# One more quarter of the first matrix by seven products, and two sums begun by a copy from bank to bank

## The chip, the cores and the metric

The kernel runs on one core of a Trainium2 chip. The metric is the device time of one execution in microseconds (us). The core's engines work side by side, each through a list of its own, and wait for one another by semaphores: TensorE (PE in the profile; its weight loads are PEld), VectorE (DVE), ScalarE (ACT), GpSimd (POOL) and SyncE (SP). The last two only start transfers here, apart from one table that POOL makes at the beginning.

## The reference

Attention with a window feeds a two-matrix layer whose activation is `h - tanh(h)`:

```python
# attention: 4 x 8 heads, 768 positions, 64 wide
scores = q @ k.T / 8 - slope[head] * dist          # kept: the 96 last positions and the 8 first ones
x = softmax(scores) @ v                            # 3072 tokens x 512
# layer
h = x @ w_in                                       # 512 -> 2048
g = h - np.tanh(h)
out = g @ w_out                                    # 2048 -> 512
```

Inputs and output are float32; the kernel multiplies in bf16 and adds up in float32.

## The kernel before

The 3072 tokens are cut into 24 tiles of 128, numbered 0 to 23 in the kernel's own order. Each goes through attention (S: scores, E: exp on ScalarE, M: mask by VectorE, AV: product with the values, R and N: division by the row sum, Xe: transposed into `xT`), then through the first matrix, `h - tanh(h)` into `gall` (th on ScalarE, g on VectorE), and the second matrix, and is stored (st).

**First matrix.** Tiles are taken in groups: 0 and 1 alone, then five pairs (groups 2 to 6), then three groups of four tiles (7: tiles 12 to 15, 8: 16 to 19, 9: 20 to 23). The 2048 columns are 16 blocks of 128. For a group of four tiles `m1.g.f` makes one block: four matmuls of 512 columns at line 477, added up in one bank. Groups 8 and 9 make blocks 4 to 15 in another way: a *unit* (g, j) is a quarter of the matrix, blocks 4j to 4j+3, and is worked out by the seven products of Strassen and Winograd (`d1` to `d7`, line 536, four matmuls of 256 columns each) on 2 x 2 blocks. They need sums of weights (`v1` to `v4` for each j, line 509) and of inputs (`y1` to `y4` for each g, line 514). A unit has three banks, r, q and z. Bank r takes M1, then M6, M5 and M3 on top, and ScalarE copies its state after M1, M6 and M5 (`e0`, `e1`, `e2`); q takes M2; z takes M7 and M4. VectorE makes the results from banks and copies: `q11` (M2 plus the copy of M1, in bank q), `q22` and `q21` (z plus a copy). Tanh and g then take two blocks at a time from two banks or from memory, 1024 elements wide (lines 562 and 568), against 512 for an m1 (lines 576 and 590).

**Second matrix.** For each pair of tiles a, a+1 the same scheme (`p1` to `p7`, line 645, eight matmuls of 256 columns each), with sums of activations made by VectorE (`n1` to `n4`, line 630) and of weights (`w1` to `w4`). Copies of bank r are `a0`, `a1`, `a2`; results are `c11` (q plus the copy of M1), `c12` (a copy of r), `c21` and `c22` (z plus a copy), each 128x256 (line 659, copies at 274 and 276).

**What sets the order.** ORDER is a list of some 980 words, written out in the file; the kernel takes them one by one and gives each to its engine (`/a` ScalarE, `/d` VectorE, `/p` POOL, `/s` SP where the operation has a choice). Nothing is moved afterwards, so an engine's list is the words of that engine in this order, and an instruction that waits holds up all behind it on its engine. HOMES gives each value its bank, its piece of the common memory `mem` or its buffer. The time of a wait thus follows from both lists. Loads of q, k and v (lq, lk, lv) are started by POOL, transposing transfers (T, Xe) by SP, stores by either.

Of the kernel before, what the change touches and what calls it, by code (L numbers as in the profile page):

```python
# [29 lines left out]
lv.6 a1.0/a c11.0 th.3.0 w3.0 p5.0 g.3.10 p7.0 a2.0/a n1.2/d th.3.4 g.3.0 p1.2 th.3.6 n2.2/d p2.2 a0.2/a w4.1 th.3.8  # L30
c22.0 p6.2 V.5/a n4.2/d T.8 p4.0 n3.2/d a1.2/a g.3.8 T.9 p5.2 g.3.6 p7.2 c21.0 a2.2/a T.10 g.3.4 st.1.0/p p3.2 M.6.1
lk.11 c11.2 S.7 c12.2/a c22.2 lv.11 n4.0/d AV.6 E.7.1 p4.2 lk.12 R.6 N.6/d E.7.0 m1.3.14 lv.9 K.7/d V.6/d M.7.1 X.6
lk.16 th.3.14 p3.0 M.7.0 Xe.6/a c21.2 lq.11 AV.7 g.3.14 c12.0/a lk.13 R.7 S.8 N.7/d lq.12 n1.4/d X.7 E.8.1 p1.4 Xe.7/d
lv.10 n2.4/d m1.4.8 K.9/a E.8.0 v1.1 st.2.0/p n3.4/d m1.4.10 th.4.8 a0.4/d lv.8 g.4.8 p6.4 th.4.10 v2.1 E.9.0 lq.13
m1.4.14 g.4.10 M.8 a1.4/a S.9 th.4.14 T.11 p5.4 g.4.14 E.9.1 V.7/d p2.4 a2.4/d E.10.0 M.9 T.12 m1.4.2 E.10.1 n4.4/d
m1.4.6 K.10/a st.0.0/s M.10 AV.9 th.4.6 m1.4.0 th.4.2 g.4.6 m1.4.4 R.9 T.13 N.9/d p7.4 g.4.2 th.4.4 Xe.9 th.4.0 g.4.4
AV.8 V.9/a p3.4 c11.4 c22.4 R.8 m1.4.12 N.8/d c12.4/a st.4.0/p g.4.0 p4.4 Xe.8 th.4.12 lq.15 v3.1 S.10 c21.4 lk.15
g.4.12 p1.6 E.12.0 lv.13 n1.6/d p2.6 n2.6/d a0.6/a lq.14 E.11.1 K.12/d AV.10 lk.14 p6.6 E.11.0 R.10 c11.6 V.10/d lq.16
m1.5.10 N.10/d a1.6/a K.11/a n4.6/d lv.12 S.11 th.5.10 n3.6/d T.15 p5.6 g.5.10 E.12.1 v1.3 m1.5.8 E.13.1 M.12 m1.5.14
a2.6/a th.5.8 T.14 M.11 m1.5.12 E.13.0 m1.5.6 v3.3 th.5.12 Xe.10 v4.1 th.5.14 g.5.12 p3.6 th.5.6 g.5.8 T.16 AV.11 g.5.14  # L40
m1.5.2 g.5.6 m1.5.0 V.11/d th.5.2 R.11 N.11/d c12.6/a p7.6 th.5.0 st.6.0/p g.5.2 Xe.11 lk.17 AV.12 g.5.0 m1.5.4 c22.6
# [11 lines left out]
lv.21 g.7.14 m1.7.13 th.7.0 T.23 g.7.11 p4.10 g.7.0 th.7.13 Xe.19 g.7.13 S.16 v4.2 p1.12 c21.10 E.20.0 K.21/d n1.12/d
p2.12 K.20/d a0.12/d E.21.0 n2.12/d AV.18 E.20.1 c11.12 p6.12 R.18 N.18/d a1.12/a n1.14/d S.17 Xe.18 n3.12/d p5.12 M.20
E.21.1 Xe.16 p7.12 a2.12/a n4.12/d E.22.0 AV.20 c22.12 p3.12 M.21 E.22.1 p4.12 K.22/a c12.12/a R.20 n2.14/d V.20/a
st.12.0/p S.18 n3.14/d lv.23 p1.14 N.20/d E.23.1 M.22 AV.21 E.23.0 d1.8.1 d2.8.1 y1.8 e0.8.1/a R.21 p2.14 y2.8 a0.14/a
N.21/d V.21/a d6.8.1 y3.8 Xe.21 AV.22 q11.8.1 e1.8.1/a m1.8.0 R.22 c21.12 N.22/d Xe.20 d5.8.1 th.8.0 d7.8.1 c11.14
e2.8.1/a y4.8 d1.8.3 g.8.0 Xe.22 d2.8.3 e0.8.3/a q22.8.1 d3.8.1 d6.8.3 M.23 th.8.4 st.11.0/s d1.8.2 p6.14 e0.8.2/a
n4.14/d V.22/a d6.8.2 g.8.4 e1.8.3/a d2.8.2 e1.8.2/a d4.8.1 q11.8.3 d5.8.3 AV.23 q21.8.1 e2.8.3/a d5.8.2 a1.14/a R.23
q11.8.2 d3.8.3 e2.8.2/a d7.8.3 N.23/d th.8.12 d3.8.2 q22.8.3 Xe.23 p5.14 th.8.6 g.8.12 d7.8.2 a2.14/a st.13.0/s m1.8.2  # L60
q22.8.2 st.8.0/s th.8.8 p3.14 g.8.6 d4.8.3 g.8.8 th.8.2 d4.8.2 c12.14/a m1.9.0 st.14.0/p y1.9 q21.8.3 m1.8.1 g.8.2
th.8.14 d1.9.1 q21.8.2 m1.8.3 e0.9.1/a y2.9 th.8.10 g.8.14 p7.14 d1.9.2 c22.14 th.8.1 d6.9.1 y3.9 d2.9.2 g.8.10 e1.9.1/a
d2.9.1 th.8.3 p4.14 g.8.1 e0.9.2/a g.8.3 d5.9.1 d6.9.2 q11.9.1 p1.16 e1.9.2/a n1.16/d e2.9.1/a d5.9.2 c21.14 a0.16/a
# [58 lines left out]
def kernel(  # L122
# [11 lines left out]
    nc = tc.nc  # L134
# [249 lines left out]
    def mask_of(u, o):  # L384
        return 2 if o else min(nth[u], 1)
# [457 lines left out]
```

## Time and profile before

| what | before |
|---|---|
| median of three runs | 201.43 us (201.39 to 201.97) |
| span of the profiled execution, first to last instruction | 199.8 us |
| PE busy | 193.1 us (97%), 2219 matmuls |
| VectorE busy | 178.6 us (89%), 348 instructions |
| ScalarE busy | 135.1 us (68%), 234 instructions |
| granted TensorE clock | 1.000 throughout |
| chain that ended last, PE's share | 85% |

The profile gives the span of its execution; the three times are of runs of the whole program and lie 1.6 us above it in the median (201.43 - 199.8). A time predicted from rows of the trace is worked out against the span, and the 1.6 us are added. Rows of groups name line, engine, operation, target and source, shapes and count, then the busy time and the mean duration of one in ns, and then the idle time of the engine ahead of them with what ended it. Rows of the chain and of the timeline give start and length in us. Rows by stretch give the length, then PE, PEld, DVE, ACT and POOL busy with instruction counts, the granted clock, the transfer engines' busy share and GB/s.

### The profile page before, as it was taken

Reading aid. Unit: us, or ns where it says so; the run is one execution under the profiler, and the core shown is the slowest. Engines: PE = TensorE matmul, PEld = TensorE weight load, DVE = VectorE, ACT = ScalarE, POOL = GpSimd, SP = SyncE. Lnnn points to the kernel's source line nnn. Section 1 sums busy time; section 2 is a strip of 40 time slices with the busy share of each in tenths; the row PEclk is TensorE's granted clock in tenths of the full one; section 3 lists DMA queues with packets and bytes.
Section 4 is the critical chain, followed back from the end, with each engine's and each line's share of the span. In section 5 each row is a group of like instructions: output and inputs, shape, how many; then the busy total and the mean of one; then the engine's idle time right before and its main releaser. Section 6 shows DMA issues by size and latency. Waiting matters only on the chain.

```text
span 199.8 us, 5524 instructions
## 1 busy us (share of the span) xinstructions
PE 193.1 (97%) x2219; PEld 157.8 (79%) x2219; DVE 178.6 (89%) x348; ACT 135.1 (68%) x234; POOL 75.3 (38%) x97
## 2 busy tenths in 40 slices
PE   8799999999999999999999999999999999999992
PEld 2469998888888988988898655688898687888892
DVE  6487599999999999999999898999999999999942
ACT  3698898726569559758947789578778777464220
POOL 8987576350694057069207904702000100001110
PEclk9999999999999999999999999999999999999999
DMA  5999999999999999989996998994733101001233
GB/s 148 211 180 185 198 163 207 201 156 141 193 167 196 178 153 135 133 188 171 137 158 146 140 173 192 154 155 85 55 108 121 66 0 54 3 0 52 107 132 131
DMA packets 103545, 27.36 MB, mean 137 GB/s; under 512 B 93920, under 2 KB 101472, under 8 KB 103520
## 3 DMA queue, kind: packets, MB, share of 16 engines
q0 software_dynamic: 74048, 16.78, 89.5%
q1 hardware_dynamic: 28928, 9.70, 27.6%
q10 hardware_dynamic: 544, 0.52, 1.0%
q8 instruction: 17, 0.28, 0.5%
q14 instruction: 8, 0.07, 0.1%
HBM read 27.26 MB, written 6.29 MB: 168 GB/s over the span
## 4 chain that ended last, share of the span: by engine, by line
PE 85%; DVE 7%; DMA 3%; ACT 2%; issue 1%; ACTq 0%; DVEq 0%
PE ps L645 36%; PE ps L477 27%; PE ps L536 9%; PE ps L396 5%; PE ps L427 5%; DMA f<-in_q_dram 3%; DVE gall L590 2%; DVE x L444 2%; DVE mem L407 1%; PE ps L455 1%; ACT mem L403 1%; PE ps L320 1%; ACT mem L274 1%; PE ps L365 1%; ACT th L576 1%
## 5 line engine op out<-in xcount | busy, mean ns | idle before, releaser
L477 PE MATMUL ps<-xT,w_in_bf 128*128 128x256 bf16 (+2 forms) x544 | 69.0, 279 | 0.0
L477 PEld LDWEIGHTS <-w_in_bf 128*128 128x128 bf16 x544 | 47.2, 98 | 12.4
L576 ACT ACTIVATE th<-ps 128x512 f32<-128x512 f32 (+1 forms) x74 | 41.8, 591 | 18.7 <-PE ps L477 13.6
L590 DVE TENSOR_TENSOR gall<-ps,th 128x512 bf16<-128x512 f32 (+1 forms) x74 | 47.4, 668 | 6.0 <-ACT th L576 5.6
L645 PEld LDWEIGHTS <-gall 128*128 128x128 bf16 x488 | 46.4, 98 | 7.0
L662 POOL DMA_DIRECT2D out_dram<-ot x14 | 8.1, 580 | 102.5 <-ACT ot L274 52.4
L403 ACT ACTIVATE mem<-ps 128x1024 bf16<-128x1024 f32 x44 | 43.3, 1024 | 4.3 <-PE ps L396 4.2
L645 PE MATMUL ps<-w_out_bf,gall 128*128 128x256 bf16 (+1 forms) x296 | 36.3, 270 | 0.0
L274 ACT COPY sn<-ps 128x256 f32<-128x256 f32 x32 | 12.0, 375 | 20.3 <-PE ps L645 16.3
L645 PE MATMUL ps<-f,ss 128*128 128x256 bf16 x192 | 24.9, 273 | 0.0
L645 PE MATMUL ps<-wc,gall 128*128 128x256 bf16 x192 | 24.9, 273 | 0.0
L342 POOL DMA_DIRECT2D vb<-in_v_dram x24 | 21.5, 900 | 2.2 <-issue 1.0
L645 PEld LDWEIGHTS <-ss 128*128 128x128 bf16 x192 | 18.3, 98 | 2.8
L342 POOL DMA_DIRECT2D mem<-in_k_dram x20 | 17.9, 899 | 4.8 <-DMA w_out_bf<-in_moe_w_out_dram 3.1
L342 POOL DMA_DIRECT2D mem<-in_q_dram x20 | 18.1, 904 | 3.8 <-DMA w_out_bf<-in_moe_w_out_dram 3.0
L412 DVE TENSOR_TENSOR mem<-mem,mk 128x2048 bf16<-128x2048 bf16 x16 | 19.2, 1215 | 0.0
L659 DVE TENSOR_TENSOR ot<-ps,sn 128x256 f32<-128x256 f32 x36 | 14.7, 415 | 3.6 <-ACT sn L274 2.5
L444 DVE TENSOR_TENSOR x<-ps,rden 128x512 bf16<-128x512 f32 x23 | 15.8, 687 | 0.5
L274 ACT COPY mem<-ps 128x512 f32<-128x512 f32 (+1 forms) x22 | 12.7, 585 | 5.1 <-PE ps L536 3.9
L427 PEld LDWEIGHTS <-mem 128*128 128x128 bf16 x352 | 13.4, 97 | 2.1 <-ACT mem L403 0.5
L427 PE MATMUL ps<-vb,mem 128*128 128x65 bf16 x352 | 14.7, 193 | 0.0
L396 PE MATMUL ps<-mem 64*128 64x128 bf16 x352 | 13.1, 217 | 0.0
(78 smaller groups left out, 220.7 us busy)
## 6 DMA issues: line engine op xcount, KB each, us to landing
out_dram<-ot POOLq DMA_DIRECT2D x14, 256.0 KB, 2.8
vb<-in_v_dram POOLq DMA_DIRECT2D x24, 128.0 KB, 6.2
mem<-in_q_dram POOLq DMA_DIRECT2D x22, 128.0 KB, 6.3
mem<-in_k_dram POOLq DMA_DIRECT2D x22, 128.0 KB, 6.1
out_dram<-ot SPq DMA_DIRECT2D x9, 256.0 KB, 2.0
w_out_bf<-in_moe_w_out_dram POOLq DMA_DIRECT2D x4, 512.0 KB, 10.7
w_in_bf<-in_moe_w_in_dram POOLq DMA_DIRECT2D x4, 256.0 KB, 7.6
w_in_bf<-in_moe_w_in_dram POOLq DMA_DIRECT2D x2, 512.0 KB, 11.0
```

The lines of the kernel that those rows point to most:

```text
L274: nc.scalar.copy(out=out, in_=in_)
L342: eng(e).dma_start(out=dst, in_=rows_of(src, u).rearrange("h p d -> p h d"))
L396: nc.tensor.matmul(bank(("s", u, o), hh)[:, p * P : (p + 1) * P], buf(("qk", back[u] if o else u))[r, 1, p, :], buf(("qk", u))[r, 0, p, :] ...
L403: nc.scalar.activation(d, banks(("s", u, o), 0, 1), AF.Exp, bias=0.0, scale=scale)
L412: nc.vector.tensor_tensor(out=t, in0=t, in1=mk[:, 1:3], op=ALU.mult)
L427: nc.tensor.matmul(t[:, h // (H // 2), h % (H // 2), :], buf(("p", u, o))[:, slot(h), :], buf(("v", back[u] if o else u))[:, h, 0 : Dh + 1 ...
L444: nc.vector.tensor_tensor(out=buf(("x", u)).rearrange("q (a h) d -> q a h d", a=2), in0=t[:, :, :, 0:Dh], in1=rden.to_broadcast([P, 2, H / ...
L477: nc.tensor.matmul(t[:, (f - f0) * n : (f - f0 + 1) * n], w_in_bf[j][:, c, fo : fo + P], x[:, c, 0:n], start=(c == 0), stop=(c == CD - 1),)
L536: nc.tensor.matmul(t[:, r * 2 * P : (r + 1) * 2 * P], w(r)[:, c], x[:, c], start=first and r + c == 0, stop=c == 1, skip_group_check=not f ...
L576: nc.scalar.activation(h_view(buf(("th", g, f0)), g, m), h_view(bank(("h", g, f0)), g, m), AF.Tanh, bias=0.0, scale=1.0)
L590: nc.vector.tensor_tensor(out=o, in0=v(h), in1=v(th), op=ALU.subtract)
L645: nc.tensor.matmul(bank((holder, a))[:, c0:c1], s(f), t(f)[:, c0:c1], start=first and f == 0, stop=f == HF - 1, skip_group_check=not first,)
```

## The change

Four things are changed, and a fifth follows from them.

- Groups 8 and 9 make blocks 0 to 3 by seven products too: two more units, (8, 0) and (9, 0), in place of `m1.8.0` to `m1.8.3` and `m1.9.0` to `m1.9.3`.
- In all eight units `e0` copies M1 from bank r to bank q, on ScalarE, and `d2` adds M2 onto it with `start` off. The sum `q11` is gone, and so are the buffers `k0`.
- In the second matrix the same is done for the pairs from tile 14 on (FORKED): `a0` copies from bank r to bank q on ScalarE, `p2` adds onto it, and `c11` becomes a copy out of bank q, by ScalarE (pairs 16, 18, 20) or VectorE (14, 22).
- The scores set `start` only on the first of the four matmuls that fill a bank.
- Buffers: three more pieces of `mem`, one `xT` less, two masks instead of three. ORDER and HOMES are written anew.

```diff
-    NM, NV, NG, NSS, NSN = 23, 12, 5, 5, 4
+    NM, NV, NG, NSS, NSN = 26, 12, 5, 5, 4
-    DUNITS = [(8, 1), (8, 2), (8, 3), (9, 1), (9, 2), (9, 3)]
+    DUNITS = [(g, j) for g in range(8, 10) for j in range(4)]
+    FORKED = range(14, NU, 2)
-    mk = pool.tile([P, 3, H, P], BF16, name="mk")
+    mk = pool.tile([P, 2, H, P], BF16, name="mk")
-    buffers("xT", 4, [P, CD, 4 * P], BF16)
+    buffers("xT", 3, [P, CD, 4 * P], BF16)
...
     def a_S(xs):
-                        buf(("qk", u))[r, 0, p, :], start=u >= BIASED, stop=u >= BIASED or p == NP - 1,
+                        buf(("qk", u))[r, 0, p, :], start=u >= BIASED and p == 0, stop=u >= BIASED or p == NP - 1,
+                        skip_group_check=u >= BIASED and p > 0,
...
     def d_keep(g, j, k):
-        return buf(("k0", g, j)) if k == 0 else mems(("k12", g, j), FP32)[:, (k - 1) * 4 * P : k * 4 * P]
+        return d_bank(g, j, "q") if k == 0 else mems(("k12", g, j), FP32)[:, (k - 1) * 4 * P : k * 4 * P]
     def in_product(g, j, k):
-            2: ("q", lambda r: w_in_of(a + r, 2), x_block(g, 2, 1), True),
+            2: ("q", lambda r: w_in_of(a + r, 2), x_block(g, 2, 1), False),
     def d_add(g, j, k):
-        if k == 0:
-            q = d_bank(g, j, "q")
-            nc.vector.tensor_tensor(out=q, in0=q, in1=d_keep(g, j, 0), op=ALU.add)
-            return
...
     def product(a, k, c0=0, c1=DH2):
-            2: ("q", lambda f: g_of(a, HF + f), w(1, 0), True),
+            2: ("q", lambda f: g_of(a, HF + f), w(1, 0), a not in FORKED),
     def keep(e, a, k):
-        copy(e, buf(("sn", a, k)), bank(("r", a))[:, 0:DH2])
+        copy(e, buf(("sn", a, k)) if k or a not in FORKED else bank(("q", a))[:, 0:DH2], bank(("r", a))[:, 0:DH2])
     def result(e, a, i, j, c0=0, c1=DH2):
-        if (i, j) == (1, 2):
-            copy(e, o, bank(("r", a))[:, c0:c1])
+        if i == 1 and (j == 2 or a in FORKED):
+            copy(e, o, bank(("qr"[j - 1], a))[:, c0:c1])
```

Of the new ORDER, engine by engine: up to p6.10 on PE, v1.2 on VectorE, V.15 on ScalarE, the store of tile 5 on POOL and T.19 on SP each list is as before. PE's list from there on, where it matters below:

```
before: ... p1.12 p2.12 AV.18 p6.12 ... p1.14 AV.21 d1.8.1 d2.8.1 p2.14 d6.8.1 AV.22 m1.8.0 d5.8.1 d7.8.1 d1.8.3 d2.8.3 d3.8.1 d6.8.3 d1.8.2 p6.14 d6.8.2 ...
        p4.16 p2.18 p7.18 p1.20 p3.18 p4.18 p2.20 p6.20 p7.20 p5.20 p2.22 p1.22 p4.20 p6.22 p7.22 p5.22 p3.20 p3.22.0 p4.22 p3.22.1
after:  ... S.16 p7.10 p1.12 AV.18 p4.10 p6.12 S.17 p2.12 p5.12 AV.20 p7.12 S.18 p3.12 p1.14 d1.8.0 d1.8.1 p4.12 d6.8.0 d6.8.1 AV.21 d2.8.1 d5.8.0 d2.8.0
        d5.8.1 AV.22 d3.8.0 d3.8.1 p6.14 p2.14 AV.23 d1.8.3 d7.8.1 p5.14 d6.8.3 d1.8.2 d7.8.0 d2.8.3 d5.8.3 d4.8.1 d7.8.3 d4.8.0 d6.8.2 d3.8.3 d4.8.3 d5.8.2
        p7.14 d1.9.0 d2.8.2 p4.14 d6.9.0 d3.8.2 p3.14 d2.9.0 d5.9.0 d1.9.1 d7.9.0 d3.9.0 d7.8.2 d6.9.1 d1.9.2 d4.9.0 d4.8.2 d5.9.1 d6.9.2 d1.9.3 d7.9.1 d2.9.2
        d5.9.2 d2.9.1 d3.9.1 d4.9.1 d6.9.3 d7.9.2 d3.9.2 d2.9.3 d5.9.3 p1.16 d7.9.3 d3.9.3 p1.18 d4.9.2 p2.16 p6.18 p2.18 d4.9.3 p6.16 p7.18 p5.16 p5.18 p7.16
        p3.16 p1.20 p1.22 p4.16 p4.18 p3.18 p2.20 p2.22 p6.22 p6.20 p5.22 p7.22 p7.20 p5.20 p4.22 p3.20 p4.20 p3.22.0 p3.22.1
```

VectorE's list ends, after: `g.9.14 n1.20 n1.22 n2.22 n2.20 c21.16 n3.22 n3.20 n4.22 c21.18 n4.20 c22.22 c22.20 c11.22 c21.22 c12.20 c21.20 c12.22.0`; `c12.22.1` is ScalarE's. Before, it ended `g.9.14 n1.20 n2.20 n3.20 n1.22 c21.16 n4.20 n3.22 c21.18 c11.18 n2.22 c22.20 c11.20 c11.22 n4.22 c21.20 c22.22 c12.22.0 c21.22 c12.22.1`. N.19 goes from ScalarE to VectorE; V.16, V.20, V.21 and V.22 go to VectorE, V.17 to ScalarE.

More of the change, by code (lines that the diff above doesn't have):

```diff
@@ L53 @@
[L53 to L57, printed above, removed]
@@ L758 @@
         for k in range(3):
-            op((f"e{k}", g, j), None, lambda e, g=g, j=j, k=k: d_copy(e, g, j, k))
-        for w, k in (("q11", 0), ("q21", 1), ("q22", 2)):
+            op((f"e{k}", g, j), None if k else ACT, lambda e, g=g, j=j, k=k: d_copy(e, g, j, k))
+        for w, k in (("q21", 1), ("q22", 2)):
             op((w, g, j), DVE, lambda e, g=g, j=j, k=k: d_add(g, j, k))
```

200 lines of the change are left out of this document (102 added, 98 removed).

## The prediction

> **What bounds the kernel now.** I read the page first: busy shares, then the slices.
>
> ```profile
> PE 193.1 (97%) x2219; PEld 157.8 (79%) x2219; DVE 178.6 (89%) x348; ACT 135.1 (68%) x234; POOL 75.3 (38%) x97
> ...
> PE   8799999999999999999999999999999999999992
> ...
> DVE  6487599999999999999999898999999999999942
> ```
>
> TensorE is full from the second slice to the last but one, and VectorE is nearly as full behind it. So I asked for busy time by stretch (columns: length, then PE, PEld, DVE, ACT, POOL).
>
> ```profile
> 109.20:124.00 14.80, 14.80 (x140) 8.49 (x138) 12.91 (x25) 12.59 (x28) 7.43 (x10) 1.00 1.73 171
> 124.00:186.00 62.00, 62.00 (x621) 50.49 (x619) 61.86 (x104) 43.00 (x72) 6.70 (x9) 1.00 0.45 69
> ```
>
> From 124 to 186 us (second row) two engines are full at once: PE 62.00 and DVE 61.86 of 62.00. Which of them sets the pace, the chain that ended last tells.
>
> ```profile
> 57.85 0.40 PE ps L455 x4
> ...
> 119.00 3.45 PE ps L477 x16
> ...
> 143.74 3.06 PE ps L536 x28
> ...
> 178.65 17.12 PE ps L645 x160
> 195.80 0.42 DVE ot L659
> 196.24 0.29 DVE ot L276
> ```
>
> Every piece between 57.85 and 195.80 is PE's. TensorE's own work is the time there, and VectorE only just keeps up: its reserve has to be read apart.
>
> **The change part by part.** Per engine the order is the same up to p6.10 on PE (108.3 to 109.4 us in this trace), v1.2 on VectorE and V.15 on ScalarE; POOL's up to the store of tile 5, SP's up to T.19. The words at the head of the order are only interleaved otherwise, so I cost them at nothing. So is the `start` flag in a_S: the same matmuls. Everything else falls in 109 to 199.8.
>
> *TensorE.* Per group the first quarter loses four m1, 16 matmuls of 512 columns, and gets one unit of seven products, 28 matmuls of 256. The chain has both: 3.45 us for x16 of L477 and 3.06 for x28 of L536. Saved 0.39 per group, **0.78 for two**. All other matmuls stay in kind and number, so no other term lies on PE.
>
> PE also has small waits that a new order can shift:
>
> ```profile
> 131.50 0.65 PE L427 MATMUL ps<-vb,mem 128*128 128x65 bf16 x16
> 132.11 1.05 PE L645 MATMUL ps<-f,ss 128*128 128x256 bf16 x8
> ...
> 139.56 0.64 PE L427 MATMUL ps<-vb,mem 128*128 128x65 bf16 x16
> 140.04 1.03 PE L536 MATMUL ps<-xT,w_in_bf 128*128 128x256 bf16 x8
> ```
>
> An AV of 16 takes 0.48 to the next start at 139.56, but 0.61 at 131.50, where p6.12 waited for VectorE: 0.13 lost. Such waits are few; I let the new order have as many, with 0.3 us either way.
>
> *The fork.* M1 is copied by ScalarE from bank r to bank q (e0, and a0 for tiles 14 to 22), and d2 or p2 adds onto it. Before, the copy went to SBUF, d2 waited for nothing, and VectorE added the two (q11, c11). Now d2 stands behind e0, as d6 already did.
>
> ```profile
> L403 ACT ACTIVATE mem<-ps 128x1024 bf16<-128x1024 f32 x44 | 43.3, 1024 | 4.3 <-PE ps L396 4.2
> ...
> L274 ACT COPY sn<-ps 128x256 f32<-128x256 f32 x32 | 12.0, 375 | 20.3 <-PE ps L645 16.3 <-DVE ot L659 3.4 <-DVE mem L509 0.5
> L274 ACT COPY mem<-ps 128x512 f32<-128x512 f32 x18 | 10.3, 585 | 4.1 <-PE ps L536 3.9
> ...
> L547 DVE TENSOR_TENSOR ps<-ps,mem 128x512 f32<-128x512 f32 x6 | 4.1, 687 | 0.0
> L550 DVE TENSOR_TENSOR mem<-ps,mem 128x512 f32<-128x512 f32 x12 | 8.2, 682 | 0.0
> ...
> L562 ACT ACTIVATE th<-mem 128x1024 f32<-128x1024 f32 x6 | 6.4, 1059 | 1.4 <-DVE mem L550 1.2 <-DVE gall L568 0.2
> ```
>
> No row has ScalarE writing a bank. Bounds: 375 ns, its copy of half the width, and 1024 ns, its pass over twice the width. VectorE takes 687 ns into a bank and 682 into SBUF, so the target changes nothing there; I take 585. The Trainium skill (Perfetto Trace Analysis, Optimizing Scalar/DVE Operations) gives ScalarE about 93 ns of access overhead on SBUF and 51 on PSUM, which would make e0 some 40 ns shorter, an estimate; the sum stays as it is, the cover below grows by that, and no run here shows it yet.
>
> What hides it:
>
> ```profile
> 145.13 0.59 ACT L274 COPY mem<-ps 128x512 f32<-128x512 f32 x1 [0.28 <-PE ps L536]
> ...
> 145.76 0.60 PE L536 MATMUL ps<-mem 128*128 128x256 bf16 x4
> ```
>
> This is e0.8.3 and then d6.8.3, which starts 0.04 after the copy's end. Two d's (0.87 us) lay between d1 and d6, and just sufficed. In the new order of PE the work between d1 and d6 is d1.8.1 and p4.12 for 8.0; p4.12 and d6.8.0 for 8.1; d7.8.1 and p5.14 for 8.3; d2.8.2 and p4.14 for 9.0; three d's for 9.1 and 9.2; six for 8.2 and 9.3. At 0.44 per d and 0.87 per p that is at least 1.31, so 0.44 us more than sufficed. Between p1 and the p2 or p6 behind a0 lies 1.31 (18) or more. Cost 0; if ScalarE comes a tanh late, see the rivals.
>
> *VectorE.* An instruction's duration is not its cost, since the next starts before it ends:
>
> ```profile
> 147.52 1.21 DVE L568 TENSOR_TENSOR gall<-ps,th 128x1024 bf16<-128x1024 f32 x1
> 148.65 0.69 DVE L547 TENSOR_TENSOR ps<-ps,mem 128x512 f32<-128x512 f32 x1
> 149.25 0.68 DVE L550 TENSOR_TENSOR mem<-ps,mem 128x512 f32<-128x512 f32 x1
> ```
>
> So 1.13 for a wide G and 0.60 for a sum, 0.88 of the duration; I take that share of the rest too.
>
> ```profile
> L590 DVE TENSOR_TENSOR gall<-ps,th 128x512 bf16<-128x512 f32 x70 | 45.8, 682 | 5.5 <-ACT th L576 5.2
> L444 DVE TENSOR_TENSOR x<-ps,rden 128x512 bf16<-128x512 f32 x23 | 15.8, 687 | 0.5
> L659 DVE TENSOR_TENSOR ot<-ps,sn 128x256 f32<-128x256 f32 x36 | 14.7, 415 | 3.6 <-ACT sn L274 2.5 <-PE ps L645 0.8
> L509 DVE TENSOR_TENSOR mem<-w_in_bf 128x512 bf16<-128x512 bf16 x5 | 2.1, 413 | 0.0
> L276 DVE COPY vb<-vb 8x512 bf16<-8x512 bf16 x6 | 2.2, 360 | 0.3 <-PE ps L427 0.3
> ```
>
> Gone: six q11, 3.60; three c11 that become ScalarE copies, 1.10; eight narrow G for four wide ones, 4.80 less 4.52. Come: four v, 1.45; four q21 and q22, 2.40; N.19 from ScalarE, 0.60; three V copies net, 1.08. Sum **+0.55**, and 0.1 for a K and exchanged copies. A V copy has its own spread:
>
> ```profile
> 122.73 0.91 POOL L342 DMA_DIRECT2D mem<-in_k_dram  x1
> ...
> 123.12 0.63 DVE L276 COPY vb<-vb 8x512 bf16<-8x512 bf16 x1
> ```
>
> That is 0.63 against a mean of 0.36, while POOL was issuing a load. V.16 now stands where POOL issues without pause, so 0.3 more is the upper bound. By the Trainium skill (SBUF — State Buffer, Who interferes with whom) such a copy and GpSimd lock each other out of a shared port, and the trace agrees with the 0.63; by it VectorE would have +0.95, and the sum below stays.
>
> VectorE's reserve:
>
> ```profile
> 182.58 1.22 DVE L568 TENSOR_TENSOR gall<-mem,th 128x1024 bf16<-128x1024 f32 x1
> ...
> 184.55 0.69 DVE L630 TENSOR_TENSOR ss<-ss,gall 128x1024 bf16<-128x1024 bf16 x1
> 184.60 1.04 PE L645 MATMUL ps<-w_out_bf,gall 128*128 128x256 bf16 x8
> ...
> 185.47 1.04 PE L645 MATMUL ps<-f,ss 128*128 128x256 bf16 x8
> ```
>
> The last G ends (182.58 + 1.22) 0.80 before p2.20 starts, n2.20 0.23 before p6.20: VectorE is a fifth of a microsecond from setting the time. The new order moves these: p1.22, p4.16, p4.18 and p3.18 stand ahead of p2.20, and from the first product that needs an n2 ten p's remain (8.72 us with the split p3.22) where twelve did (10.5). I cost VectorE's extra 0.65 at nothing on that ground.
>
> *ScalarE* has 43.00 busy of 62.00: six copies, three c11, less eight tanh for four wide ones, N.19 and three V come out near even. *Queues.* POOL now has st.12 ahead of lv.23, and st.12 waits for c12.12, which ScalarE does behind e0.8.1.
>
> ```profile
> vb<-in_v_dram POOLq DMA_DIRECT2D x1, 128.0 KB, 3.6
> ...
> vb<-in_v_dram POOLq DMA_DIRECT2D x24, 128.0 KB, 6.2
> ```
>
> The first row is lv.23 alone (137 to 146 us), the second all. From p4.12 to AV.23 PE has 6.2 us; c12.12 ends some 0.7 into it, the store's issue takes 0.6: 4.9 needed with 3.6, 7.5 with 6.2. The transfer share there is the low one (0.45), so I take 3.6: nothing; otherwise +1.3. st.10, ahead of lk.23 before, now stands far behind it, so T.23 comes earlier.
>
> *Tail.*
>
> ```profile
> 195.60 0.61 PE L645 MATMUL ps<-w_out_bf,gall 128*128 128x128 bf16 x8
> ```
>
> c21.22 no longer ends behind PE, but the last copy started at 196.24, only once p3.22.1 (this row) had drained at 196.21, and still must; it is ScalarE's now, between 0.29 (VectorE's here) and 0.37 (ScalarE's at twice the width). The store after it is the same. 0, bounds -0.15 to +0.1.
>
> Sum against the profiled execution: its span of 199.8 becomes **199.0**. The runs' median of 201.43 lies 1.6 above that span; what lies around it stays: **200.65**, or -0.39%.
>
> **The rivals.** *VectorE takes over.* For: the 0.23 us. Up to n2.22, now the first that PE needs, VectorE has 0.65 more, n1.22 ahead (0.60), and lacks the relief of two of the three c11, which stood behind that point anyway (0.74): 185.24 + 2.0 = 187.2. Ten p's and 0.16 of drain: 196.1 where PE ended at 196.2. So **201.3**, the gain eaten. Against: it holds only if VectorE idles as before in 109 to 124 (1.89 of 14.80 us).
>
> *Slower: VectorE idles more at the start of the stretch.* All 16 G of group 7 now stand in one run behind their tanhs, as do the M's of 17 to 19 behind their exps; should the idle grow by half (0.95), nothing behind gives it back, since VectorE is full to 186: 201.3 + 0.95 = **202.3**. It decides from 0.7 of added idle. Against: the sums n1.12 to n3.12 and the M's with ready inputs stand close behind, so that a late tanh moves work rather than losing it.
>
> *ScalarE late at the fork.* If two of the six tight units find it inside a wide tanh (1.06 us) with 0.44 more cover than it needs, 2 x 0.6 = 1.2 is lost: **201.85**. The cover speaks against it, six units of before with less lost nothing. That the fork costs ScalarE 1024 ns a copy would end alike.
>
> *lv.23 late*: **201.95**, as worked out.
>
> **How the numbers follow.** Forecast 0.66 (own range 200.2 to 200.95 by the small waits and the tail), VectorE takes over 0.14, fork 0.08, slower 0.08, lv.23 0.04. 0.3% is 0.60 us, about what a measurement of this kernel can tell from no change: faster is under 200.83, which nine tenths of the first case give, and a little of the second: 0.62; slower is over 202.03: the slower rival and half of lv.23, 0.10; the rest 0.28. The range takes in the first two cases with their bounds, 200.1 to 201.7; the other three, 0.20 together, lie above it.
>
> **What would show it.** L477 has 64 matmuls of 512 columns instead of 96, L536 224 of 256 instead of 168; the PE pieces between 109 and the end shrink by 0.78 and the chain stays PE's. A chain that goes over L590, L630 or L550 of VectorE in 127 to 187 means VectorE took over; PE waiting on a copy of L274 at L536 is the fork; on L342, lv.23. The bank-to-bank copy should stand in its own row near 585 ns. I am wrong if PE's products do shrink and the end does not come earlier.

## The result, and the profile after

The changed kernel took 201.03 us in the median of eight runs (200.05 to 203.5) against 201.72 us (201.39 to 202.71) for the kernel before on the same chip. Two of the eight, of 203.13 and 203.5 us, ran at a lower granted clock (0.992 and 0.990, the others 0.997 to 1.000); without them the ratio is 0.9949, with a 95% interval of 0.9925 to 0.9973. Measured once more, beside 35 runs of the kernel before, it was 0.9939 (0.9913 to 0.9965). The forecast of 200.65 against 201.43 was a ratio of 0.9961, which lies inside both intervals. So the time came out as forecast, or a little better. The reasons did not all hold.

The profiled execution of the changed kernel happens to be the longest of those compared (span 199.6 us, the others 198.2 to 199.5), so it may show waits that others lack. The one of the kernel before is long too: 199.8 us, where its later runs have 199.5 in the median. (So the 1.6 us that the forecast put between span and median is less than the 1.7 to 2.2 by which one execution's time exceeds its own span; the forecast difference does not depend on it.) The changed kernel's page, busy shares:

```profile
PE 191.2 (96%) x2239; PEld 159.2 (80%) x2243; DVE 178.9 (90%) x348; ACT 135.2 (68%) x227; POOL 76.2 (38%) x99
```

TensorE has 1.9 us less, VectorE 0.3 more. Part of the 1.9 is only missing from the trace: four matmuls are not recorded (2239 against 2243 weight loads). Line numbers have shifted: L478 is m1, L537 a d, L642 a p, L396 S, L428 AV, L656 a c, L565 and L587 the wide and the narrow g, L559 and L573 their tanhs. By stretch (length, then PE, PEld, DVE, ACT, POOL busy, the granted clock, the transfer engines' share, GB/s):

```profile
109.20:124.00 14.80, 14.64 (x137) 8.38 (x138) 14.61 (x28) 11.54 (x21) 9.56 (x12) 1.00 2.05 146
124.00:142.00 18.00, 17.50 (x212) 13.29 (x210) 16.26 (x34) 13.92 (x23) 2.84 (x5) 1.00 0.83 133
142.00:186.00 44.00, 44.00 (x436) 39.29 (x436) 43.80 (x67) 30.36 (x50) 3.37 (x6) 1.00 0.22 53
```

VectorE, which idled for 1.89 us between 109 and 124 before, is now busy for 14.61 of 14.80 there; between 124 and 142 both engines have holes (0.50 and 1.74); from 142 on both are full. The groups that answer to the change's parts, from 109 us on:

```profile
L478 PE MATMUL ps<-xT,w_in_bf 128*128 128x512 bf16 x61 | 14.3, 379 | 0.2
...
L274 ACT COPY mem<-ps 128x512 f32<-128x512 f32 x16 | 9.2, 586 | 4.5 <-PE ps L537 4.5
...
L274 ACT COPY ps<-ps 128x512 f32<-128x512 f32 x8 | 4.6, 590 | 1.2 <-PE ps L537 1.2
...
L274 ACT COPY ps<-ps 128x256 f32<-128x256 f32 x5 | 1.7, 367 | 2.1 <-DVE gall L565 2.1
```

L478 has 64 matmuls of 512 columns (61 recorded and three missing). The copy from bank to bank takes 590 ns at 512 columns and 367 at 256, where the copy to memory takes 586. The chain of waits, which had no other engine between 57.85 and 195.80 before, now leaves TensorE once:

```profile
132.35 5.97 DMA xT<-x
...
140.54 1.14 DVE mem L413
...
141.73 0.80 PE ps L428 x16
```

That is the transpose Xe.18, 5.97 us from issue to landing, then M.21 on VectorE, which stands behind y1.8, the sum that waits for Xe.18, then AV.21. A second wait stands at S.16 (timeline, with the idle time ahead of the instruction in brackets):

```profile
127.71 0.84 PE L396 MATMUL ps<-mem 64*128 64x128 bf16 x24 [0.43 <-DMA mem<-mem]
```

S.16 needs the transpose T.20, which stands behind T.21 on SP in the new order, and T.21 waits for the load of q of its tile. To see what these waits are worth, take TensorE's time from the start of p6.10, up to which its list is as before, to its last matmul's end. Before, in its first profile:

```profile
108.32 1.04 PE L645 MATMUL ps<-f,ss 128*128 128x256 bf16 x8
...
195.60 0.61 PE L645 MATMUL ps<-w_out_bf,gall 128*128 128x128 bf16 x8
```

And in the second:

```profile
108.26 1.04 PE L645 MATMUL ps<-f,ss 128*128 128x256 bf16 x8
...
195.54 0.61 PE L645 MATMUL ps<-w_out_bf,gall 128*128 128x128 bf16 x8
```

Both give 87.89 us (195.60 + 0.61 - 108.32, and the same for the other, which is from the last experiment below). The changed kernel in its first profile, with the row of AV.23 between:

```profile
108.30 1.04 PE L642 MATMUL ps<-f,ss 128*128 128x256 bf16 x8
...
147.36 0.65 PE L428 MATMUL ps<-vb,mem 128*128 128x65 bf16 x16
...
195.10 1.06 PE L642 MATMUL ps<-w_out_bf,gall 128*128 128x128 bf16 x16
```

That is 87.86: in this execution nothing was left of the 0.78 us, because about as much went into the two waits. Yet over all runs the kernel is 1.0 us faster. The question for the experiments was therefore twofold: where does TensorE's gain go, and how much of the end is TensorE's at all?

### The profile page after: what moved, and what is told of

It is laid out like the page before. It is cut to its first block, busy times and chain, and to the rows that moved or that the text cites. A ratio compares the mean times of both kernels' runs of the same rounds, so it can differ in the third digit from the quotient of the medians.

```text
span 199.6 us, 5563 instructions
## 1 busy us (share of the span) xinstructions
PE 191.2 (96%) x2239; PEld 159.2 (80%) x2243; DVE 178.9 (90%) x348; ACT 135.2 (68%) x227; POOL 76.2 (38%) x99
## 4 chain that ended last, share of the span: by engine, by line
PE 74%; DVE 9%; DMA 7%; POOL 4%; ACT 2%; issue 2%; DVEq 0%; POOLq 0%; ACTq 0%
PE ps L642 32%; PE ps L478 23%; PE ps L537 11%; DMA w_in_bf<-in_moe_w_in_dram 4%; PE ps L428 4%; PE ps L396 3%; DMA xT<-x 3%; DVE gall L587 2%; POOL vb L342 2%; DVE x L445 2%; DVE mem L408 2%; POOL mem L339 2%; ACT th L573 1%; ACT mem L404 1%; DVE ot L656 1%
## 5 line engine op out<-in xcount | busy, mean ns | idle before, releaser
L478 PE MATMUL ps<-xT,w_in_bf 128*128 128x256 bf16 (+2 forms) x509 | 60.6, 272 | 1.2 <-DMA w_in_bf<-in_moe_w_in_dram 1.0
L478 PEld LDWEIGHTS <-w_in_bf 128*128 128x128 bf16 x512 | 44.0, 98 | 11.4 <-DMA w_in_bf<-in_moe_w_in_dram 1.2
L642 PEld LDWEIGHTS <-gall 128*128 128x128 bf16 x488 | 46.2, 98 | 6.1
L573 ACT ACTIVATE th<-ps 128x512 f32<-128x512 f32 (+1 forms) x66 | 37.2, 585 | 17.5 <-PE ps L478 14.8
L587 DVE TENSOR_TENSOR gall<-ps,th 128x512 bf16<-128x512 f32 (+1 forms) x66 | 41.9, 665 | 6.0 <-ACT th L573 5.6
L659 POOL DMA_DIRECT2D out_dram<-ot x16 | 9.1, 571 | 98.3 <-DVE ot L656 45.5
L642 PE MATMUL ps<-w_out_bf,gall 128*128 128x256 bf16 (+1 forms) x296 | 35.9, 270 | 0.0
L642 PE MATMUL ps<-wc,gall 128*128 128x256 bf16 x192 | 24.6, 273 | 0.0
L642 PE MATMUL ps<-f,ss 128*128 128x256 bf16 x192 | 24.4, 273 | 0.0
L274 ACT COPY sn<-ps 128x256 f32<-128x256 f32 x26 | 9.8, 376 | 19.5 <-PE ps L642 19.4
L642 PEld LDWEIGHTS <-ss 128*128 128x128 bf16 x192 | 18.3, 98 | 2.8
L445 DVE TENSOR_TENSOR x<-ps,rden 128x512 bf16<-128x512 f32 x24 | 16.5, 688 | 0.7 <-DMA xT<-x 0.3
L428 PEld LDWEIGHTS <-mem 128*128 128x128 bf16 x352 | 13.4, 97 | 2.6 <-DVE mem L413 0.5
L274 ACT COPY mem<-ps 128x512 f32<-128x512 f32 (+1 forms) x20 | 11.5, 586 | 5.5 <-PE ps L537 4.5
L428 PE MATMUL ps<-vb,mem 128*128 128x65 bf16 x352 | 14.8, 193 | 0.3 <-ACT mem L404 0.2
L656 DVE TENSOR_TENSOR ot<-ps,sn 128x256 f32<-128x256 f32 x31 | 12.6, 414 | 2.6 <-ACT sn L274 1.7
L537 PE MATMUL ps<-mem 128*128 128x256 bf16 x96 | 13.7, 273 | 0.0
## 6 DMA issues: line engine op xcount, KB each, us to landing
w_out_bf<-in_moe_w_out_dram POOLq DMA_DIRECT2D x4, 512.0 KB, 10.7
```

What stands on the lines that cost most here:

```text
L274: nc.scalar.copy(out=out, in_=in_)
L428: nc.tensor.matmul(t[:, h // (H // 2), h % (H // 2), :], buf(("p", u, o))[:, slot(h), :], buf(("v", back[u] if o else u))[:, h, 0 : Dh + 1 ...
L445: nc.vector.tensor_tensor(out=buf(("x", u)).rearrange("q (a h) d -> q a h d", a=2), in0=t[:, :, :, 0:Dh], in1=rden.to_broadcast([P, 2, H / ...
L478: nc.tensor.matmul(t[:, (f - f0) * n : (f - f0 + 1) * n], w_in_bf[j][:, c, fo : fo + P], x[:, c, 0:n], start=(c == 0), stop=(c == CD - 1),)
L537: nc.tensor.matmul(t[:, r * 2 * P : (r + 1) * 2 * P], w(r)[:, c], x[:, c], start=first and r + c == 0, stop=c == 1, skip_group_check=not f ...
L573: nc.scalar.activation(h_view(buf(("th", g, f0)), g, m), h_view(bank(("h", g, f0)), g, m), AF.Tanh, bias=0.0, scale=1.0)
```

## The experiments

### The changed kernel again

No edit.

> The changed kernel once more, nothing edited. Its undisturbed runs lay between 200.05 and 201.58 us, wider than the kernel before (201.39 to 202.12), and the profiled one was the longest. Theory (transfers): the spread comes from two transfers that land late in some executions only, the transpose T.20 that S.16 waits for (0.49 us of TensorE in the profiled run) and Xe.18 that the sum y1.8 waits for (0.95 us of VectorE). Then this profile shows waits of another size at those two places, and its span follows them: 198.2 to 198.7 where both are short, 199.5 where both are long. Rival (VectorE): the time is set by VectorE's list from 142 us on, which is the same in every execution; then the waits at those two places differ and the span does not follow, or the waits are the same in each. Ratio to before either way 0.993 to 0.997.

Measured: 200.78 us, ratio 0.9939 (0.9913 to 0.9965). Its profile:

```profile
107.89 1.04 PE L642 MATMUL ps<-f,ss 128*128 128x256 bf16 x8
110.07 0.42 DVE L656 TENSOR_TENSOR ot<-ps,sn 128x256 f32<-128x256 f32 x1 [0.81 <-ACT mem L404]
...
112.38 1.88 DVE L587 TENSOR_TENSOR gall<-ps,th 128x512 bf16<-128x512 f32 x3
...
113.71 0.60 PE L396 MATMUL ps<-mem 64*128 64x128 bf16 x15 [0.38 <-DVE gall L587]
...
146.77 0.65 PE L428 MATMUL ps<-vb,mem 128*128 128x65 bf16 x16
...
194.50 1.06 PE L642 MATMUL ps<-w_out_bf,gall 128*128 128x128 bf16 x16
```

Neither of the two waits is there, but a third one is, at S.15, and the span is 199.0 us, longer than was expected without the two. S.15 waits for the banks that g.7.15 and g.7.0 read, the first two of the three g's in the row of 112.38; these came late on VectorE, since VectorE had stood still ahead of c11.10 for 0.81 us. (The brackets name ScalarE, long done; c11.10 writes the output buffer of tile 10, from which the store of tile 9 had still to be read. The same instruction names that store in the next experiment.) From p6.10 to the end it is 87.67. So the theory named the right kind of cause, transfers that land early or late, but a place too few. From AV.23 to the last products both executions have 47.74 us and 47.73 (195.10 - 147.36, 194.50 - 146.77).

### T.20 ahead of T.21

```diff
- ... M.18 AV.19 T.21 th.7.3 m1.7.9 v2.2 R.19 m1.7.11 g.7.8 T.20 th.7.9 ...
+ ... M.18 AV.19 T.20 T.21 th.7.3 m1.7.9 v2.2 R.19 m1.7.11 g.7.8 th.7.9 ...
```

> T.20 stands ahead of T.21 on SP, whose inputs land 3 us earlier; nothing else moves. Transfers: T.20 is issued near 117 us and lands near 121 as in the kernel before; T.21 still waits for lq.21 (120.2) and becomes the last that S.16 needs, landing near 123 to 125; S.16's wait of 0.49 us on TensorE is gone, 0.3 to 0.5 us less than the changed kernel in executions that had it, 0.2 in the median. Rival (VectorE): S.16 starts earlier, but AV.18, N.18, Xe.18 and y1.8 hang on VectorE's list, and the end moves by less than 0.1.

Measured: 201.19 us, 0.9966 (0.994 to 0.9991); no faster. In its profile S.16 no longer waits, but S.15 does, as in the execution above:

```profile
109.94 0.42 DVE L656 TENSOR_TENSOR ot<-ps,sn 128x256 f32<-128x256 f32 x1 [0.57 <-DMA out_dram<-ot]
...
113.82 0.60 PE L396 MATMUL ps<-mem 64*128 64x128 bf16 x15 [0.39 <-DVE gall L587]
```

T.20 now lands at 122.6, but T.21 behind it only at 127.4, 7.7 us after its issue and as late as T.20 landed in the two executions above (127.7 and 127.3); 123 to 125 was expected. Taking one late transfer away brings no gain where another one is as late.

### Xe.18 without company

```diff
- ... AV.18 n2.12/d ... st.11.0/p n1.14/d p2.12 st.8.0/p K.22/a E.21.1 M.20 lv.22 ...
+ ... AV.18 lv.22 n2.12/d ... st.11.0/s n1.14/d p2.12 st.8.0/s K.22/a E.21.1 M.20 ...
```

> The stores of tiles 11 and 8 go to SP behind the transpose Xe.18, and POOL's load lv.22 goes to behind AV.18, 3 to 4 us earlier, so that POOL starts nothing while Xe.18 is under way. Transfers: Xe.18 lands in 2 to 3.5 us instead of 6; y1.8's wait on VectorE (0.95) falls below 0.2, the waits of AV.21 and AV.22 on TensorE (0.55 together) go, and the kernel is 0.4 to 0.9 us faster than the changed one in executions that had them. Rival (the transfer is slow by itself, since three transposes are issued back to back): it lands as late and nothing moves. Second rival: the moved load and stores delay Xe.16 or Xe.17 instead, and y1.8 waits as long.

Measured: 201.62 us, 0.9997 (0.9973 to 1.002): slower than the changed kernel by some 0.9 us. Transfers between 128 and 140 us in the changed kernel (issues, KB, median us to landing):

```profile
out_dram<-ot POOLq DMA_DIRECT2D x2, 256.0 KB, 4.7
...
xT<-x SPq DMA_TRANSPOSE x3, 3.7
```

And in this one:

```profile
out_dram<-ot SPq DMA_DIRECT2D x3, 256.0 KB, 4.7
...
xT<-x SPq DMA_TRANSPOSE x3, 3.7
```

The stores take as long on the other queue, and so do the transposes; Xe.18 itself takes 5.7 us against 5.97, and y1.8 still waited 0.7. So Xe.18 is as slow when POOL starts neither store. Whether the stores delay it from either queue, or the two transposes ahead of it do, is not shown: in the next run, which has the stores on SP too, it takes 4.1. Of the 0.9 us that the whole kernel lost, some 0.4 show at the end: from TensorE's last matmul to the end of the span it is 3.8 us here and in the next run, 3.4 in the changed kernel. The rest this profile does not settle.

### Both

The two edits together.

> The two edits together. Transfers: span 198.0 to 198.6 in each execution, spread no wider than the kernel before's (0.7 us), 0.9915 to 0.994 of before. Rival (VectorE): no better than the changed kernel, 0.994 to 0.997.

Measured: 201.36 us, 0.998 (0.995 to 1.0009). T.21 landed at 129.5 in the profiled execution and S.16 waited 1.3 us for it; this execution was the longest of its twelve. The theory that repairing these two late transfers by such edits pays has fallen. That an execution's length follows where they land is borne out here, but no run isolates it.

### One product less

```diff
     def product(a, k, c0=0, c1=DH2):
+        if (a, k) == (14, 3):
+            return
```

> The changed kernel without the product p3.14 (eight matmuls of 256 columns, 0.87 us of TensorE at 158 us); tiles 14's second half of the result lacks that product, everything else is made. VectorE's and ScalarE's lists are untouched. Theory (TensorE's matmuls set the end from 142 us on): 0.7 to 0.9 us faster than the changed kernel, 0.9895 to 0.991 of before. Rival (VectorE, at its limit as g_twice shows, paces the end just as much: p6.18 and p6.22 start 0.06 us after the sums they need): TensorE comes earlier and waits there, 0 to 0.2 us faster, 0.993 to 0.995, and its profile shows waits of 0.8 us in all between 159 and 188, at p6.18 or before.

Measured: 200.36 us, 0.9929 (0.9907 to 0.9951). Against the 0.9939 and 0.9949 of the changed kernel that is 0.2 to 0.4 us, of 0.87 taken out, and within the intervals nothing. The profile is the sharper witness (L644 is a p here):

```profile
107.92 1.04 PE L644 MATMUL ps<-f,ss 128*128 128x256 bf16 x8
...
146.00 0.65 PE L428 MATMUL ps<-vb,mem 128*128 128x65 bf16 x16
...
156.30 1.06 ACT L559 ACTIVATE th<-mem 128x1024 f32<-128x1024 f32 x1 [0.33 <-DVE gall L565]
157.26 0.57 ACT L274 COPY mem<-ps 128x512 f32<-128x512 f32 x1
...
157.88 0.60 PE L537 MATMUL ps<-mem 128*128 128x256 bf16 x4 [0.25 <-ACT mem L274]
...
159.55 0.60 PE L537 MATMUL ps<-xT,mem 128*128 128x256 bf16 x4 [0.20 <-ACT mem L274]
...
193.74 1.06 PE L644 MATMUL ps<-w_out_bf,gall 128*128 128x128 bf16 x16
```

From AV.23 to the last products it is 47.74 us (193.74 - 146.00), with eight matmuls less the same as with them. What TensorE saved at 157 us it spent within 6 us, most of it (0.8 us from start to start; the brackets count from the modelled ends) waiting for e1.9.0 and e2.9.0, copies of ScalarE. The rival's waits are there, at d5.9.0 and d3.9.0 and not at p6.18. They are not only lost cover between a product and its copy: e1.9.0 (the row of 157.26) starts 11.26 us after AV.23, and 11.25 in the first profile of the changed kernel (158.61 - 147.36), since th.8.6 ahead of it waits 0.33 us for VectorE in both. Taking the product out did not bring ScalarE or VectorE forward.

This execution had none of the three waits ahead of 142 us, so it shows what the change can do there: from p6.10 to the end 86.88 us (193.74 + 1.06 - 107.92), 1.01 less than before. None of that 1.01 is the missing product's, if the whole kernel would again need 47.74 behind AV.23, as in both of its profiles. No profile of the changed kernel itself lacks the waits, but its shortest runs have the same span: 198.0 and 198.2 us, 198.2 here. By stretch, this run and then the second profile of the kernel before (of the last experiment):

```profile
109.20:124.00 14.80, 14.80 (x139) 8.50 (x138) 14.47 (x29) 11.59 (x21) 9.07 (x11) 1.00 2.18 161
124.00:142.00 18.00, 18.00 (x231) 14.42 (x229) 17.41 (x36) 13.78 (x23) 3.51 (x5) 1.00 0.60 132
...
109.20:124.00 14.80, 14.80 (x139) 8.44 (x138) 12.96 (x24) 12.57 (x28) 7.37 (x10) 1.00 1.75 174
124.00:142.00 18.00, 18.00 (x226) 14.06 (x225) 17.97 (x36) 13.95 (x23) 5.57 (x7) 1.00 1.13 119
```

VectorE (the third of the busy times) idles for 0.92 us up to 142 us here, 0.33 and 0.59, and for 1.87 before. In the first profile of the changed kernel it is 1.93, 0.19 and 1.74.

### VectorE loaded by one wide g

```diff
- ... e2.8.2/a g.8.12 p4.14 ...
+ ... e2.8.2/a g.8.12 g.8.12 p4.14 ...
```

> g.8.12 (wide, 128x1024) is made twice in a row by VectorE, at about 157 us: 1.13 us more on VectorE and nothing else. The prediction priced 0.65 us more on VectorE at nothing, so a reserve of that size must have been there before. Theory (reserve used up): in the profile of the changed kernel n2.18 ends 0.06 us ahead of p6.18 and n2.22 0.06 ahead of p6.22, so 0.9 to 1.1 us slower than the changed kernel, 0.9985 to 1.000 of before. Rival (reserve left, as what waits can be done later): 0 to 0.3 slower, 0.994 to 0.996.

Measured: 202.13 us, 1.0007 (0.9975 to 1.0038): 0.6% above the changed kernel, or 1.2 us for 1.13 added. There is no reserve. The way it takes is in the timeline around the doubled instruction (now one row of two):

```profile
155.66 2.48 DVE L565 TENSOR_TENSOR gall<-ps,th 128x1024 bf16<-128x1024 f32 x2
...
158.24 1.06 ACT L559 ACTIVATE th<-mem 128x1024 f32<-128x1024 f32 x1 [1.65 <-DVE gall L565]
...
159.20 0.57 ACT L274 COPY mem<-ps 128x512 f32<-128x512 f32 x1
...
159.82 0.60 PE L537 MATMUL ps<-mem 128*128 128x256 bf16 x4 [0.69 <-ACT mem L274]
```

th.8.6 waits for the tanh buffer that g.8.12 reads, e1.9.0 stands behind th.8.6 on ScalarE, and d5.9.0 waits for e1.9.0. So VectorE reaches TensorE through ScalarE's list, not only through the sums n2. In the changed kernel the same tanh waits as well, for 0.33, and TensorE does not:

```profile
157.65 1.06 ACT L559 ACTIVATE th<-mem 128x1024 f32<-128x1024 f32 x1 [0.33 <-DVE gall L565]
```

### Each e0 twice

```diff
- ... d1.8.0 y2.8 d1.8.1 M.21 e0.8.0 p4.12 e0.8.1 ...
+ ... d1.8.0 y2.8 d1.8.1 M.21 e0.8.0 e0.8.0 p4.12 e0.8.1 e0.8.1 ...
```

and so for all eight units.

> Each of the eight copies from bank to bank e0 is made twice in a row by ScalarE: 0.48 us more between d1 and the d6 and d2 that wait for it, eight times. The prediction gave the fork 0.44 us of cover beyond need. Theory (cover): losses of 0.05 to 0.65 at the tight units only (8.0 and 8.1, which stand in a row, and 8.3), 0.1 to 0.7 us slower than the changed kernel, 0.9945 to 0.9975 of before. Rival (the fork is tight, as what ScalarE does later comes late for VectorE, which has no reserve): 0.3 per unit or more, over 1.5 us slower, above 1.001.

Measured: 203.71 us, 1.0082 (1.0056 to 1.0108): 1.4% or 2.8 us above the changed kernel. The fork is tight. A second copy holds up what stands behind it for longer than the 0.48 us assumed: e0.9.1 and its double take 1.21, where the single one takes 0.61 in the changed kernel (the row of 161.07 further down).

```profile
161.47 1.21 ACT L274 COPY ps<-ps 128x512 f32<-128x512 f32 x2
```

Who waited (us in total, times, longest):

```profile
PE ps L537 <- ACT ps L274: 1.6, 5, 0.5
```

The row is new: TensorE behind the copy from bank to bank, five times. In the changed kernel unit (9, 1) shows how little was left:

```profile
160.13 0.60 PE L537 MATMUL ps<-xT,w_in_bf 128*128 128x256 bf16 x4
...
160.81 0.38 ACT L274 COPY ot<-ps 128x256 f32<-128x256 f32 x1
...
161.07 0.61 ACT L274 COPY ps<-ps 128x512 f32<-128x512 f32 x1
...
161.44 1.04 PE L537 MATMUL ps<-mem 128*128 128x256 bf16 x8
```

The first row is d1.9.1, whose results are there at 160.73. ScalarE was then about to start c12.14, so e0.9.1 began only at 161.07 and ended at 161.68. The last row holds d7.8.2 and d6.9.1, so d6.9.1 starts 0.44 after 161.44, at 161.88: 0.2 us to spare.

### Without the fork

```diff
-        return d_bank(g, j, "q") if k == 0 else mems(...)
+        return buf(("k0", g, j)) if k == 0 else mems(...)
-            2: ("q", lambda r: w_in_of(a + r, 2), x_block(g, 2, 1), False),
+            2: ("q", lambda r: w_in_of(a + r, 2), x_block(g, 2, 1), True),
     def d_add(g, j, k):
+        if k == 0: ...   # q11: q + k0 into q, by VectorE, ahead of the unit's first tanh
```

> In the eight units e0 copies to memory again and VectorE adds it to bank q (q11, ahead of the unit's first tanh); d2 starts its bank. All else as changed, the pairs' a0 included. VectorE gets eight sums at 0.60: 4.8 us more in 144 to 184. Theory (VectorE is at its limit): nearly all of it goes to the end, 3 to 4.8 us slower than the changed kernel, 1.009 to 1.018 of before. Rival (VectorE has a reserve of some us hidden in its list, as TensorE alone sets the end): under 1 us slower, below 0.999.

Measured: 209.94 us, 1.0398 (1.0343 to 1.0454): 4.5% or 9 us above the changed kernel for 4.8 us of sums. By stretch:

```profile
142.00:186.00 44.00, 37.60 (x353) 31.97 (x351) 40.08 (x63) 25.57 (x42) 2.54 (x5) 1.00 0.20 46
```

All three engines stand still at times: the tanh waits for the sum (10.7 us in seven waits), g waits for the tanh, the next products for the copies behind the tanh. Each wait is handed round. More than the sums' own time is lost, and how much of that is due to a q11 ill placed, this run can't tell. (Line numbers are two higher in this run.)

### The first quarter back to m1

```diff
-    DUNITS = [(g, j) for g in range(8, 10) for j in range(4)]
+    DUNITS = [(g, j) for g in range(8, 10) for j in range(1, 4)]
- ... d1.8.0 ... d6.8.0 ... d7.8.0 ... d4.8.3 ... d1.9.0 ... d6.9.0 ... d2.9.0 ... d4.9.0 ...
+ ... m1.8.0 ... m1.8.1 ... m1.8.2 ... d4.8.3 m1.8.3 ... m1.9.0 ... m1.9.1 ... m1.9.2 ... m1.9.3 ...
```

> The first quarter of groups 8 and 9 goes back to m1, four matmuls of 512 columns per block, with narrow tanh and g; the six other units, the fork and the new order stay. TensorE gets 0.78 us more (2 x (3.45 - 3.06)). VectorE loses four v (1.3) and four q (2.4) and gets eight narrow g for four wide ones (0.3): 3.4 us less. Theory (TensorE's list sets the end): 0.6 to 0.9 us slower than the changed kernel, so 0.997 to 0.9985 of before where the changed kernel has 0.994. Rival (VectorE sets the end from 142 us on, since in the profile of the changed kernel p6.18 and p6.22 start 0.06 us after the sums n2.18 and n2.22 they need): the 3.4 us given back outweigh the 0.78, and it is as fast as the changed kernel or faster, 0.991 to 0.995.

In this first form two banks were overwritten before their tanh and g had read them, so two blocks of group 8 and 9 take another block's numbers. Measured: 203.18 us, 1.0065 (1.003 to 1.0101). With other banks, and with m1.9.2, m1.9.3 and some tanhs and g's moved up, each block is read before its bank is written again:

> The first quarter of groups 8 and 9 goes back to m1 (four matmuls of 512 columns per block, narrow tanh and g), in banks of its own; six units, the fork and the new order stay. TensorE gets 0.78 us more (2 x (3.45 - 3.06)), VectorE 3.4 less (no v and q of those units 3.7, eight narrow g for four wide ones 0.3), ScalarE 1.9 less (six copies 2.9, eight narrow tanh for four wide ones 1.0). Theory (TensorE's matmuls set the end, the other two only follow): 0.6 to 0.9 us slower than the changed kernel, 0.997 to 0.9985 of before where the changed kernel has 0.994. Rival (VectorE and ScalarE pace the end, since g_twice and e0_twice cost 1.2 and 2.8 us): as fast as the changed kernel or faster, below 0.9955.

Measured: 203.78 us, 1.0098 (1.0061 to 1.0135): 3.1 us above the changed kernel, beyond both theories. In its profile TensorE waits between 142 and 166 us (line numbers are one lower: L536 is a d, L427 an AV):

```profile
PE ps L536 <- ACT ot L273: 0.5, 1, 0.5
PE ps L427 <- DVE x L444: 0.5, 1, 0.5
PE ps L536 <- DVE gall L586: 0.4, 1, 0.4
```

Between 142 and 186 us TensorE is busy for 42.39 of 44.00, where the changed kernel has it full: 1.6 us lost at new places beside the 0.78 of matmuls. It is an inconclusive test of the 0.78: the words around the first quarter were ordered for seven products, and taking them out makes others late, although VectorE and ScalarE have less to do. It suggests that the order belongs to its work.

### An attempt at a faster version

```diff
- ... lv.17 ... lq.20 ... lq.23 ... lv.19 ... lk.20 ... lq.22 ... lk.22 ... lk.21 ... lq.21 ...
+ ... lv.17 ... lq.20 lk.20 ... lv.19 lk.21 lq.21 ... lq.22 ... lk.22 lq.23 ...
- ... v3.2 m1.7.0 V.16/d a1.10/a R.16 K.17/d lq.22 N.16/d ... g.7.15 ... T.21 ... T.20
+ ... v3.2 m1.7.0 a1.10/a g.7.15 R.16 K.17/d lq.22 N.16/d ... th.7.0 V.16/a ... T.20 T.21
```

> Three edits ahead of 128 us, where each profile of the new order shows TensorE waiting 0.6 to 1.0 us at S.15 or S.16: POOL loads q and k of tiles 20 and 21 ahead of those of 22 and 23; T.20 stands ahead of T.21 on SP; on VectorE g.7.15 stands ahead of R.16, K.17 and N.16, and V.16 goes to ScalarE, so that the bank S.15 waits for is free 1 us sooner. Theory (these waits are VectorE's and the transposes' lateness): both waits fall below 0.2 and the kernel is 0.3 to 0.7 us faster than the changed one, 0.9905 to 0.9925 of before. Rival (the transfer engines are full from 109 to 131 us and VectorE from 142 on, so what is moved up here is lost again there): 0.993 to 0.9965, as the changed kernel.

Measured: 206.66 us, 1.0224 (1.0179 to 1.0268). The load of tile 21 now goes to the piece of memory from which K.17 had still to read, so K.17 takes other keys than it should, and waits for the load:

```profile
DVE mem L276 <- DMA mem<-in_k_dram: 4.0, 1, 4.0
PE ps L396 <- DVE x L445: 3.3, 1, 3.3
```

VectorE stands still for 4.0 us, S.15 for 3.3 behind it. The run says nothing about the waits it was meant to remove. No version was found that beats the changed kernel.

### The kernel before again

No edit.

> The kernel before, unedited, for a second profile of it: from the start of p6.10 to that of p3.22.1 the first one has 87.28 us of TensorE, 0.3 of them waits, while the profiles of the changed kernel have 87.30 and 87.12, 0.9 to 1.0 of them waits. Theory (the change takes 0.78 us of matmuls away and the waits ahead of 142 us give back 0.6 in the executions that were profiled): this profile shows 87.1 to 87.5 again, with waits of 0.2 to 0.5. Rival (before has such waits as well and the first profile was a lucky one): 87.8 or more. Ratio 0.998 to 1.002.

Measured: 201.66 us, 0.9998 (0.9979 to 1.0016). Its 87.89 us from p6.10 to the end stand above; the rival that the first profile was a lucky one has fallen. In it the store of tile 9 landed at 110.19, later than in any profile of the new order, and cost nothing, since c11.10 stood at 110.74 there: the new order has it up to 1.7 us earlier.

## Why the prediction was right or wrong

**TensorE, -0.78: right.** Matmuls and counts came out as priced. In the execution without waits ahead of 142 us (the one without p3.14) the stretch from p6.10 is 1.01 us shorter than before; by the prices 0.78 is the matmuls' and the rest would be the few waits of before. No run isolates the 0.78: in the one that put m1 back it is buried under new waits.

**Small waits, "as many, 0.3 either way": mis-sized.** Before has 0.3 us of them, in both profiles. The changed kernel has hardly any to 1.0, by execution: S.15 behind the store of tile 9 (0.6), S.16 behind T.20 (0.4), AV.21 behind Xe.18 (0.4). The step that failed is the reading of the queues: it looked at lv.23 and T.23, but not at T.20, which moved behind T.21 on SP, nor at c11.10, which moved up to the landing of a store. These waits go with what an execution gains: nothing in the first profile, 1.0 us in the one without them.

**The fork, cost 0: right, but not for the reason given.** 590 ns against the 585 taken. From the overheads that the Trainium skill (Perfetto Trace Analysis, Optimizing Scalar/DVE Operations) gives for ScalarE, 93 ns on SBUF and 51 on PSUM, the estimate was a copy some 40 ns shorter than one to memory; the rows have 590 against 586, so here it isn't, and the measurement decides. The cover was counted on TensorE alone, from d1 to d6, "0.44 more than sufficed". But e0 does not start when d1 ends: ScalarE had other work in front, and 0.2 us was left at (9, 1). Doubling the copies cost 2.8 us, where by the cover 0.7 at most was expected; that each second copy took 0.60 and not 0.48 adds 1.0 to that at most (eight times 0.12), which is still less than 2.8.

**VectorE's 0.65 at nothing: right in the sum, wrong in the reserve.** The ground given was that more p's stand ahead of the sums n2. It is VectorE's idle time that the gain goes with. Up to 142 us it is 1.92 before; 1.93 in the first profile, where it only moved behind 124 us and the stretch from p6.10 gained 0.03; 1.58 in the second, which gained 0.22; and 0.92 in the execution that gained 1.01. A reserve there is not: 1.13 us more cost 1.2, and 0.87 less on TensorE brought nothing after AV.23. From there to the last products the executions have 47.74 us with p3.14 and without. Around 157 us TensorE, ScalarE and VectorE run in step, tied by tanh buffers and copies. That is the rival "VectorE takes over" in kind. Its condition was that VectorE idles as before, and in the first profile, where it does, the gain is gone as the rival has it; over all runs it is not. Whether the 1.0 us is due to TensorE's matmuls or to VectorE's shorter idle time, no run separates.

**The slower rival:** VectorE's idle between 109 and 124 fell, from 1.89 to between 0.2 and 0.9, instead of growing. **lv.23:** landed 3.5 us after its issue, and AV.23 did not wait; right. **V.16 beside POOL:** 0.58 us in the first profile, while POOL issued a load, and 0.28 or less for the V copies on VectorE behind it: the upper bound. By the Trainium skill (SBUF — State Buffer, Who interferes with whom) the two engines lock each other out of a shared port at such a copy; the trace agrees again.

**Tail, 0 (-0.15 to +0.1):** 0.2 less, just past its lower bound. From the last matmul's end to the span's end it was 3.6 us before (199.8 - 196.21) and 3.4 after (199.6 - 196.16). **The head of the order, nothing:** p6.10 starts at 108.26 and 108.32 before and between 107.74 and 108.74 in eight profiles of the new order, so no difference shows.

So an execution with no late transfer gains some 1.2 us (1.01 and the tail, read from the run without p3.14), the first profile 0.2 (199.6 against 199.8), and the runs' 1.0 and 1.2 lie toward the upper end. That the forecast's 0.78 came so near is in part luck: VectorE had no reserve to pay the 0.65 from, and it idled less than was assumed in most executions profiled, while waits that the forecast had not seen took part of the gain back.

## What to carry to other kernels

A chain that shows one engine from end to end does not prove that this engine alone sets the time: take a little work off it, and add a little to its neighbour, before pricing a change by it. Cover for a copy has to be read on the engine that makes the copy, from when that engine is free, not from when the data is there. And a reordering has to be searched for every instruction that comes closer to the landing of a transfer; such waits come and go from one execution to the next, so one profile shows only some of them.

## What was not expected of the hardware

A bank-to-bank copy on ScalarE costs what a copy to memory costs (590 and 586 ns for 128x512, 367 and 378 for 128x256). The same transfers landed very differently in executions whose order is the same up to there: Xe.18 3.4 us after its issue (without p3.14) to 6.0 (first profile), the store of tile 9 2.6 to 4.3 (in the same run and in the second profile). What makes the difference is not shown. AV.23 starts 38.08 us after p6.10 where they land early and 39.06 in the first profile.
